# Later bounds of w_in and later tables of scales while attention runs alone

## The chip, the cores and the metric

The kernel runs on one core of a Trainium2 chip. The metric is the device time of one execution in microseconds (us), lower is better. The engines of a core work side by side, each through its own list of instructions in order: TensorE (PE in the profile; PEld is its weight load), VectorE (DVE), ScalarE (ACT), GpSimd (POOL), and SyncE (SP), which issues the DMAs.

## What is computed

Attention over 8 batches of 8 heads, followed by a feed-forward layer (FFN) on its output. Each head has 512 local and 32 global positions of 64 elements. Global queries see all keys; a local query sees the global keys and the local ones at most 32 places away.

```python
s_g = scale * q_g @ k_all.T;  out_g = sm(s_g) @ v_all
s_ll = where(|i - j| <= 32, scale * q_l @ k_l.T, -1e9)
out_l = sm(concat(scale * q_l @ k_g.T, s_ll)) @ concat(v_g, v_l)
x = concat(out_g, out_l)                  # 4608 tokens x 512
h = x @ w_in                              # 512 x 2048
g = where(h > 0, h, exp(min(h, 0)) - 1)
out = g @ w_out                           # 2048 x 512
```

## The kernel before

**Two streams.** attention() is a generator that issues the attention slot by slot; ffn_stream() issues the FFN for blocks of 256 tokens as they become ready. The main loop (the last lines of attn_ffn) takes one step of attention, and, by the table PACE, as many steps of the FFN as are due. For its first 66 steps attention runs alone: lead[0] is true, and the FFN stream issues no products. A slot has four steps, S, V, T and U. S computes scores (L685 and L689 for the global queries, L734 for the local ones), and the softmax follows: maxima on VectorE (L696 and L697, or L746), exponentials on ScalarE (L701, L703, L752), the reciprocal of the sum on VectorE (L756, L757), the product with it on GpSimd (L758, L710 for the global part). T, two slots later, transposes p on TensorE (L789) and copies it to the tile pt on VectorE (L791). U does the same for the global probabilities pg (L721 on TensorE, L722 on ScalarE, into the same pt). V, three slots later, multiplies pt with v (L795); ScalarE copies the output to xr (L828), and VectorE takes up the global part and the maximum (L833 or L835, L837). In the same steps, while attention is alone, L918 issues products of zeros on TensorE as fillers.

**The weights.** w_in and w_out come as 64-bit floats. They are turned into two float16 parts each, high and low, in units of 1 MB; unit(m, p, raw) does this for w_in (m = 0) or w_out (m = 1). Its pieces are put off by defer(n, fn): tick() counts steps, and fn is called n ticks later. s0 (L184 on ScalarE, L185 on GpSimd), s1a to s1c (L189, L192, L196 on VectorE) and s1d (L200 on ScalarE, which also gives each partition's maximum, the bound) rebuild 32-bit floats. For w_in, s2 spreads the bound over the partitions: all_max() transposes it on TensorE into a bank of PSUM (L137) and reduces it on VectorE (L138). s3 makes a power of two of it (L127, L128, L132) and writes the high part on ScalarE (L209, the tiles winh and wouth); s4 writes the low part on VectorE (L212, winl and woutl).

```python
lag = 7 if m else 16
for i, fn in ((1, s0), (1 + d, s1a), ..., (1 + 4 * d, s1d),
              (1 + lag, s2), (2 + lag, s3), (3 + lag, s4)):
    defer(i, fn)
```

**The tables.** When a group of weights has its last unit issued, load_weights() defers tables(group): L228 and L229 multiply the powers of w_in and w_out and take the maximum; five ticks later rest() spreads it by all_max (wm_a, wm_b) and makes the group's scales (L233, L234, L235). The FFN can start on a group when its tables exist; scales() (L579 to L583 on GpSimd) makes the scales of a block from them.

In the first 66 steps four units are issued, by UNITS: w_in and w_out of group a in steps 1 and 8, w_in and w_out of group b in steps 18 and 30. The later ones (groups c to e) are issued when, or shortly before, the FFN runs beside attention.

**What sets the order.** Engines work in order, but the order is set when the program is built: the Tile framework schedules by its own estimate of when an instruction can start, so that an operation that is deferred by a step can change places with several others. Tiles of the pool ps_a (named pa, four banks of PSUM) are shared by scores, transposes and all_max. Raw weights have two buffers, so that a load waits on SyncE's queue until L200 of the unit two before is done, and the loads of k, q and v behind it wait too.

Of the kernel before, what the change touches and what calls it, by code (L numbers as in the profile page):

```python
# [61 lines left out]
def attn_ffn(ctx: ExitStack, tc: tile.TileContext, qT, qgT, kT, vT, w_in, w_out, mask, out):  # L62
# [23 lines left out]
    def defer(n, fn):  # L86
        if n == 0:
            return fn()
        later.setdefault(now[0] + n, []).append(fn)
# [10 lines left out]
    lead = [True]  # L100
# [23 lines left out]
    def power(dst, src):  # L124

        dst = dst.bitcast(I32)
        nc.vector.tensor_scalar(dst, src.bitcast(I32), 0x7f800000, None, ALU.bitwise_and)  # L127
        nc.vector.tensor_scalar_max(dst, dst, LOW)  # L128

    def inverse(dst, src):  # L130

        nc.vector.tensor_scalar(dst.bitcast(I32), src.bitcast(I32), TOP, -1.0, ALU.subtract, ALU.mult)  # L132

    def all_max(dst, src):

        tp = ps_a.tile([P, 512], F32, name="pa")
        tc.keep_in_program_order(nc.tensor.transpose(tp[:, 0:P], src.to_broadcast([P, P]), ident))  # L137
        nc.vector.tensor_reduce(out=dst, in_=tp[:, 0:P], op=ALU.max, axis=AX.X)  # L138
# [15 lines left out]
    def load_weights():  # L154
        todo = [(group, m, p) for group in "abcde" for p in range(*GROUPS[group]) for m in range(2)]
        raws = [fetch(*todo[0][1:])]
        yield
        for n, (group, m, p) in enumerate(todo):
            if n + 1 < len(todo):
                raws.append(fetch(*todo[n + 1][1:]))  # L160
            unit(m, p, raws[n])
            if (m, p) == (1, GROUPS[group][1] - 1):
                defer(12, lambda group=group: tables(group))
                if p == NP - 1:
                    defer(13, lambda: tables("f"))
            yield

    def fetch(m, p):
        raw = ffn.tile([P, NC, 2 * P, 2] if m == 0 else [P, 2, DM, 2], I32, name="raw")
        nc.sync.dma_start(raw, w1[:, :, 2 * p * P:2 * (p + 1) * P, :] if m == 0 else w2[:, 2 * p:2 * p + 2, :, :])  # L170
        return raw

    def unit(m, p, raw):
        f = slice(2 * p * P, 2 * (p + 1) * P)
        shape = [P, NC, 2 * P] if m == 0 else [P, 2, DM]
        parts = [w[:, :, f] for w in win] if m == 0 else [w[:, 2 * p:2 * p + 2, :] for w in wout]
        pw = (pww if m == 0 else pwo)[:, p:p + 1]
        u = ffn.tile(shape, F32, name="cu", bufs=3)
        mx = ffn.tile([P, 4], F32, name="cm", bufs=4)
        high, low = raw[..., 1], raw[..., 0]  # L180
        ui = u.bitcast(I32)

        def s0():
            nc.scalar.activation(u, high.bitcast(F32), AF.Abs)  # L184
            nc.gpsimd.tensor_scalar(u, u, FMAX, FMIN, ALU.min, ALU.max)  # L185

        def s1a():
            tc.keep_in_program_order(
                nc.vector.tensor_scalar(ui, ui, 3, 0x3ffffff8, ALU.logical_shift_left, ALU.bitwise_and))  # L189

        def s1b():
            nc.vector.scalar_tensor_tensor(out=ui, in0=high, scalar=-0x40000000, in1=ui,  # L192
                                           op0=ALU.bitwise_and, op1=ALU.bitwise_or)

        def s1c():
            nc.vector.scalar_tensor_tensor(out=ui, in0=low, scalar=29, in1=ui,  # L196
                                           op0=ALU.logical_shift_right, op1=ALU.bitwise_or)

        def s1d():
            nc.scalar.activation(low.bitcast(F32), u, AF.Abs, accum_out=mx[:, m:m + 1])  # L200

        def s2():
            if m == 0:
                all_max(mx[:, 1:2], mx[:, 0:1])

        def s3():
            power(pw, mx[:, 1:2])
            inverse(mx[:, 3:4], pw)
            nc.scalar.activation(parts[0], u, AF.Copy, scale=mx[:, 3:4])  # L209

        def s4():
            nc.vector.scalar_tensor_tensor(out=parts[1].rearrange("p a b -> p (a b)") if m else parts[1],  # L212
                                           in0=u.rearrange("p a b -> p (a b)") if m else u, scalar=mx[:, 3:4],
                                           in1=parts[0].rearrange("p a b -> p (a b)") if m else parts[0],
                                           op0=ALU.mult, op1=ALU.subtract)

        d = 1 if lead[0] else 2
        lag = 7 if m else 16
        for i, fn in ((1, s0), (1 + d, s1a), (1 + 2 * d, s1b), (1 + 3 * d, s1c), (1 + 4 * d, s1d),
                      (1 + lag, s2), (2 + lag, s3), (3 + lag, s4)):  # L220
            defer(i, fn)

    def tables(group):

        r = slice(*GROUPS[group])
        wm = wts.tile([P, 4], F32, name=f"wm_{group}")
        t = wts.tile([P, NP], F32, name=f"t_{group}")
        nc.vector.tensor_mul(t[:, r], pww[:, r], pwo[:, r])  # L228
        nc.vector.tensor_reduce(out=wm[:, 0:1], in_=t[:, r], op=ALU.max, axis=AX.X)  # L229

        def rest():
            all_max(wm[:, 1:2], wm[:, 0:1])
            nc.vector.reciprocal(wm[:, 2:3], wm[:, 1:2])  # L233
            nc.vector.tensor_scalar(t[:, r], pwo[:, r], wm[:, 2:3], 8.0, ALU.mult, ALU.mult)  # L234
            nc.vector.tensor_scalar_mul(isc[:, r], pww[:, r], -2.0 ** -28)  # L235
            tab[group] = wm[:, 1:2], t

        defer(5, rest)
# [731 lines left out]

    f = ffn_stream()
    units = load_weights()
    done = credit = 0

# [108 lines left out]
```

## Time and profile before

| | us |
|---|---|
| three runs | 920.2, 917.78, 920.91 (median 920.2) |
| profiled execution | 918.45 |
| its span, first to last instruction | 916.6 |
| TensorE busy | 878.5 (96%) |
| VectorE busy | 703.1 (77%) |
| ScalarE busy | 637.2 (70%) |
| GpSimd busy | 177.4 (19%) |
| mean granted clock of TensorE | 0.996 |

A row of a time line gives start, duration, engine, line, operation, output and inputs, shapes, the number of merged instructions, and in brackets the idle time of the engine ahead of it with what ended it. A row of a stage gives its length, then busy time and number of instructions of PE, PEld, DVE, ACT and POOL, then the granted clock of TensorE (1.00 is full speed), the share of the DMA engines and GB/s. Numbers of buffers are left out in the profile, so that the tiles of different slots have one name.

### The profile page before, as it was taken

To read this page: it belongs to the slowest core of one execution; us is meant where nothing else is said; L and a number is where in the kernel's file an instruction comes from. 1 tells how busy PE (TensorE), PEld (TensorE's weight loads), DVE (VectorE), ACT (ScalarE), POOL (GpSimd) and SP (SyncE) were. 2 spreads that over 40 slices of the span, in tenths; PEclk is the share of its full clock that TensorE was granted. 3 is DMA by queue.
4 is the path that set the end of the run, shared out by engine and by line. 5 is a ranking of instruction groups with operands and counts; after the bars stand their busy time and mean duration, and the time that the engine had idled before them with its cause. 6 is when DMAs were issued, how large, how long until landed. Compare 5 with 4: busy or idle time off the path is not lost.

```text
span 916.6 us, 26268 instructions
## 1 busy us (share of the span) xinstructions
PE 878.5 (96%) x10791; PEld 719.0 (78%) x10791; DVE 703.1 (77%) x1949; ACT 637.2 (70%) x1458; POOL 177.4 (19%) x237
## 2 busy tenths in 40 slices
PE   7989888899999999999999999999999999999997
PEld 3557565566666888888888888888888888888886
DVE  5997998898689768686877768777868677766566
ACT  5789987876667667676767577676766676756664
POOL 3352554332212001011101011110110011200000
PEclk9899999999999999999999999999999999999999
DMA  7978866626643134104401134114410111000000
GB/s 264 369 267 286 292 210 219 200 89 210 196 144 103 71 128 154 50 24 130 174 24 51 70 128 154 50 60 138 154 35 37 48 48 48 1 25 24 1 25 24
DMA packets 41776, 108.32 MB, mean 118 GB/s; under 512 B 4152, under 2 KB 6840, under 8 KB 41656
## 3 DMA queue, kind: packets, MB, share of 16 engines
q1 hardware_dynamic: 41368, 106.38, 33.7%
q8 instruction: 85, 1.39, 0.6%
q14 instruction: 35, 0.29, 0.1%
q10 hardware_dynamic: 288, 0.26, 0.1%
HBM read 89.33 MB, written 17.30 MB: 116 GB/s over the span
## 4 chain that ended last, share of the span: by engine, by line
PE 33%; DVE 32%; ACT 25%; issue 4%; DMA 4%; POOL 0%; DVEq 0%; SPq 0%; ACTq 0%; POOLq 0%
PE pa L317 12%; ACT p L752 6%; ACT gh L355 6%; PE acc L476 6%; DVE gl L339 5%; DVE gx L336 5%; PE h L476 4%; ACT g L327 3%; ACT g L329 3%; DVE gx L350 2%; PE acc L441 2%; PE h L317 2%; DVE gx L351 2%; PE pa L795 2%; DVE cu L196 1%
## 5 line engine op out<-in xcount | busy, mean ns | idle before, releaser
L317 PEld LDWEIGHTS <-winh 128*128 128x128 f16 x2160 | 208.8, 98 | 32.4 <-issue 2.5
L317 PE MATMUL pa<-xh,winh 128*128 128x256 f16 x824 | 224.8, 273 | 1.4 <-DVE xglob L865 1.4
L317 PE MATMUL pa<-xh,winl 128*128 128x256 f16 x824 | 224.6, 273 | 0.0
L317 PE MATMUL pa<-xl,winh 128*128 128x256 f16 x824 | 224.6, 273 | 0.0
L355 ACT ACTIVATE gh<-gx,xs 128x896 f16<-128x896 f32 x103 | 107.5, 1044 | 133.3 <-DVE gx L352 133.3
L339 DVE SCALAR_TENSOR_TENSOR gl<-gx,xs,gh 128x896 f16<-128x896 f32 x103 | 122.6, 1191 | 73.8 <-ACT gh L355 73.8
L476 PEld LDWEIGHTS <-gh 128*128 128x128 f16 x1456 | 140.2, 98 | 19.5 <-issue 3.6
L758 POOL TENSOR_TENSOR p<-p,sm 128x512 f32<-128x512 f32 x64 | 71.4, 1118 | 330.0 <-DVE sm L757 301.8
L752 ACT ACTIVATE p<-p,m 128x128 f32<-128x128 f32 x256 | 99.3, 391 | 25.2 <-DVE m L746 25.0
L317 PEld LDWEIGHTS <-winl 128*128 128x128 f16 x1080 | 105.7, 98 | 12.6
L476 PE MATMUL acc<-wouth,gl 128*128 128x256 f16 x312 | 85.1, 273 | 1.2 <-DVE gl L339 1.1
L476 PE MATMUL acc<-wouth,gh 128*128 128x256 f16 x312 | 85.2, 273 | 0.0
L476 PE MATMUL acc<-woutl,gh 128*128 128x256 f16 x312 | 85.0, 273 | 0.0
L329 ACT ACTIVATE g<-g 128x512 f32<-128x512 f32 x135 | 85.0, 630 | 0.0
L476 PEld LDWEIGHTS <-gl 128*128 128x128 f16 x728 | 71.2, 98 | 11.5 <-DVE gl L339 3.3
L327 ACT ACTIVATE g<-pa,xs 128x512 f32<-128x512 f32 x103 | 70.2, 682 | 10.7 <-PE pa L317 10.0
L476 PE MATMUL h<-raw,gh 128*128 128x256 f16 x416 | 74.2, 273 | 0.0
L317 PE MATMUL h<-xh,winh 128*128 128x256 f16 x256 | 69.9, 273 | 0.0
L317 PE MATMUL h<-xl,winh 128*128 128x256 f16 x256 | 69.8, 273 | 0.0
L317 PE MATMUL h<-xh,winl 128*128 128x256 f16 x256 | 69.8, 273 | 0.0
L795 PEld LDWEIGHTS pa<-pt,v 128*64 128x64 f32 x1728 | 52.9, 138 | 8.0 <-issue 6.2
L336 DVE SCALAR_TENSOR_TENSOR gx<-g,p 128x512 f32<-128x512 f32 x52 | 35.9, 690 | 27.8 <-ACT g L329 26.3
(230 smaller groups left out, 1893.4 us busy)
## 6 DMA issues: line engine op xcount, KB each, us to landing
v<-vT SPq DMA_DIRECT2D x64, 512.0 KB, 4.5
k<-kT SPq DMA_DIRECT2D x32, 640.0 KB, 5.2
q<-qT SPq DMA_DIRECT2D x32, 256.0 KB, 5.8
raw<-w_in SPq DMA_DIRECT2D x8, 1024.0 KB, 5.6
raw<-w_out SPq DMA_DIRECT2D x8, 1024.0 KB, 5.9
od<-o SPq DMA_DIRECT2D x32, 256.0 KB, 2.6
o<-od SPq DMA_DIRECT2D x32, 256.0 KB, 3.0
out<-o SPq DMA_DIRECT2D x32, 256.0 KB, 2.3
```

Source lines behind the costliest of these rows:

```text
L317: nc.tensor.matmul(h[:, j, :], wt[:, c, f], xt[:, c, :], start=k == 0, stop=k == 11)
L327: nc.scalar.activation(g, hf, AF.Relu, scale=sc[:, p:p + 1])
L329: nc.scalar.activation(g, g, AF.Exp, scale=-1.0)
L336: nc.vector.scalar_tensor_tensor(out=out, in0=ins[0], scalar=-1.0, in1=ins[1], op0=ALU.add, op1=ALU.max)
L339: nc.vector.scalar_tensor_tensor(out=dst, in0=src, scalar=sg, in1=hi, op0=ALU.mult, op1=ALU.subtract)
L350: nc.vector.tensor_add(gx[:, 2:4, :], q[:, 0:2], q[:, 2:4])
L351: nc.vector.tensor_sub(gx[:, 5:7, :], q[:, 0:4:2], q[:, 1:4:2])
L355: nc.scalar.activation(gh, gx, AF.Copy, scale=sg)
L476: nc.tensor.matmul(cols, gt, w, start=p == 0 and k == 0, stop=last and k == len(todo) - 1, skip_group_check=True)
L752: nc.scalar.activation(ps[i], ps[i], AF.Exp, bias=m[:, i:i + 1], scale=-1.0, accum_out=s[:, 0, i:i + 1])
L758: nc.gpsimd.tensor_tensor(out=pp, in0=pp, in1=s[:, 1, :].unsqueeze(2).to_broadcast([P, 4, P]), op=ALU.mult)
L795: nc.tensor.matmul(o[:, to:to + n], st["v", g, t][:, 4 * h + w, :], st["pt", g, t][:, h, at:at + n], start=start, stop=True, skip_group_ch ...
```

## The change

While lead[0] is true, s2, s3 and s4 of a unit of w_in come six steps later (lag 22 in place of 16), and tables(group) eight steps later (20 in place of 12). This concerns the units of w_in of groups a and b and the tables of these two groups. s0 to s1d, the units of w_out and all units that are issued later keep their steps.

```diff
             if (m, p) == (1, GROUPS[group][1] - 1):
-                defer(12, lambda group=group: tables(group))
+                defer(20 if lead[0] else 12, lambda group=group: tables(group))
...
         d = 1 if lead[0] else 2
-        lag = 7 if m else 16
+        lag = 7 if m else 22 if lead[0] else 16
```

In the built program the order on SyncE is the same. On TensorE, VectorE, ScalarE and GpSimd it differs within attention's first 66 steps, and is the same behind them. Three places follow.

VectorE before, in the middle of attention's time alone. pt_676 is the copy of the transposed p of a slot of the first batch (the row at 40.76 us in the trace); cu_626 is the unit of w_out of group b, cm_402 the bound of w_in of group b:

```order
L756 TENSOR_SCALAR sm_591<-sm_591 128x4
L791 COPY pt_676<-pa_677 128x2x4x64
L757 RECIPROCAL sm_591<-sm_591 128x4
L189 TENSOR_SCALAR cu_626<-cu_626 128x1024
L138 TENSOR_REDUCE cm_402<-pa_683 128x1
L192 SCALAR_TENSOR_TENSOR cu_626<-raw_399,cu_626 128x1024
L127 TENSOR_SCALAR pww_114<-cm_402 128x1
L756 TENSOR_SCALAR sm_661<-sm_661 128x4
L196 SCALAR_TENSOR_TENSOR cu_626<-raw_399,cu_626 128x1024
```

VectorE now, at the same place. cu_620 is the same unit of w_out, pt_676 the same copy, and wm_a_559 the maximum for the tables of group a:

```order
L756 TENSOR_SCALAR sm_585<-sm_585 128x4
L746 ISA p1_84,m_654<-acc_637,msk_75 128x128
L746 ISA m_654 128x1
L757 RECIPROCAL sm_585<-sm_585 128x4
L138 TENSOR_REDUCE wm_a_559<-pa_660 128x1
L189 TENSOR_SCALAR cu_620<-cu_620 128x1024
L233 RECIPROCAL wm_a_559<-wm_a_559 128x1
L235 TENSOR_SCALAR isc_116<-pww_114 128x1
L192 SCALAR_TENSOR_TENSOR cu_620<-raw_396,cu_620 128x1024
L234 TENSOR_SCALAR t_a_560<-pwo_115,wm_a_559 128x1
L196 SCALAR_TENSOR_TENSOR cu_620<-raw_396,cu_620 128x1024
L791 COPY pt_676<-pa_677 128x2x4x64
```

The copy pt_676 has moved from ahead of L189, L192 and L196 of this unit to behind them.

TensorE now, around the product that reads pt_676 (h_725). pa_698 is the second bank of the scores of a later slot, p0_83 the next p to be transposed; k_632 belongs to the second batch:

```order
L734 MATMUL pa_698<-k_247,q_324 32x128 x4
L789 MATMUL pa_754<-ident_76,p0_83 128x128 x4
L795 MATMUL h_725<-pt_676,v_535 64x32 x2
L795 MATMUL h_725<-pt_676,v_535 64x64 x4
L795 MATMUL h_725<-pt_676,v_535 64x32 x4
L795 MATMUL h_725<-pt_676,v_535 64x64 x4
L795 MATMUL h_725<-pt_676,v_535 64x32 x2
L918 LDWEIGHTS wouth_91
L918 MATMUL h_749<-wouth_91 128x512
L721 MATMUL pa_766<-ident_76,pg1_82 128x128
```

Before, the product on pt_676 stood ahead of the transposes of p0_83, with a filler among its instructions; now it is behind them.

VectorE before, around the global maxima of the first batch's second half (mg_438):

```order
L229 TENSOR_REDUCE wm_a_416<-t_a_417 128x1
L235 TENSOR_SCALAR isc_116<-pww_114 128x1
L212 SCALAR_TENSOR_TENSOR woutl_92<-cu_227,cm_228,wouth_91 128x1024
L212 SCALAR_TENSOR_TENSOR winl_90<-cu_156,cm_157,winh_89 128x4x256
L696 TENSOR_REDUCE mg_438<-pa_424 128x1
```

Now, at the same place (mg_426):

```order
L757 RECIPROCAL sm_345<-sm_345 128x4
L138 TENSOR_REDUCE cm_157<-pa_480 128x1
L212 SCALAR_TENSOR_TENSOR woutl_92<-cu_227,cm_228,wouth_91 128x1024
L696 TENSOR_REDUCE mg_426<-pa_413 128x1
L696 TENSOR_REDUCE mg_426<-pa_412 128x1
```

winl of group a and the small steps ahead of it have gone from in front of the maxima; they stand now behind the maxima of the next two slots' local scores. The second winl (group b) stood in front of the maxima of the second batch, and is now behind them.

## The prediction

> **What bounds the kernel now.** I read the page first, then busy time by stage, then the time lines of VectorE (DVE), TensorE (PE), ScalarE (ACT) and GpSimd (POOL) in the stretch that the change touches, then the granted clock in windows of 3.41 us.
>
> The page: TensorE is busy nearly all the time, VectorE for three quarters.
>
> ```profile
> span 916.6 us, 26268 instructions
> PE 878.5 (96%) x10791; PEld 719.0 (78%) x10791; DVE 703.1 (77%) x1949; ACT 637.2 (70%) x1458; POOL 177.4 (19%) x237
> ```
>
> By stage (length, then busy time and instructions of PE, PEld, DVE, ACT, POOL, then granted clock, DMA share, GB/s):
>
> ```profile
> 30.00:69.00 39.00, 35.12 (x693) 23.27 (x693) 35.38 (x166) 30.14 (x109) 19.05 (x29) 1.00 0.84 307
> 200.00:400.00 200.00, 195.73 (x2356) 154.84 (x2354) 159.44 (x418) 134.98 (x324) 38.39 (x58) 1.00 0.37 123
> 400.00:916.00 516.00, 504.68 (x6217) 445.90 (x6215) 372.13 (x1015) 342.04 (x743) 53.35 (x73) 1.00 0.19 65
> ```
>
> From 200 us on TensorE is 98% busy (195.73 of 200; 504.68 of 516). Attention alone ends where the first FFN job stands:
>
> ```profile
> 68.89 0.27 PE L317 MATMUL h<-xh,winh 128*128 128x256 f16 x1
> ```
>
> Up to there many TensorE instructions are fillers (L918), and VectorE is the fullest engine doing needed work: 35.38 of 39.00 us from 30 on. Behind 69 us the change leaves the order of every engine as it is (SyncE's from the start, and the moved steps issue no DMA), and nothing there hangs on an absolute time: each transfer is issued when a buffer comes free. So what attention alone loses or gains I carry to the end one for one. The question is when the start ends.
>
> **Part 1: the bounds leave the stretch before 30 us.** The transpose that spreads the first bound of w_in is the place that the change seems to be about:
>
> ```profile
> 21.42 0.47 PE L137 MATMUL pa<-ident,cm 128*128 128x128 f32 x1 [1.58 <-ACT raw L200]
> 23.63 2.09 PE L685 MATMUL pa<-k,qg 64*32 64x256 f32 x8 [0.46 <-ACT pt L722]
> 30.01 0.42 PE L685 MATMUL pa<-k,qg 64*32 64x256 f32 x4
> ```
>
> TensorE waits 1.58 us for it. It would not start much earlier without it: what stands next, the transposes of p, needs GpSimd's p, which ends at 21.02 (19.02 + 2.00):
>
> ```profile
> 19.02 2.00 POOL L758 TENSOR_TENSOR p<-p,sm 128x512 f32<-128x512 f32 x1
> 41.70 1.30 POOL L758 TENSOR_TENSOR p<-p,sm 128x512 f32<-128x512 f32 x1 [1.09 <-DVE sm L757]
> ```
>
> So at most 0.4 us is won there, and it is lost again at 30 us: the second half of the global scores needs a block of k that is issued at 21.81 and takes 7.6 us.
>
> ```profile
> 30.01 0.12 PEld L685 LDWEIGHTS pa<-k,qg 64*32 64x32 f32 x4 [0.64 <-DMA k<-kT]
> ```
>
> ```profile
> 21.39 0.38 SPq L170 DMA_DIRECT2D raw<-w_in  x1
> 21.81 0.50 SPq L660 DMA_DIRECT2D k<-kT  x1
> ```
>
> ```profile
> k<-kT SPq DMA_DIRECT2D x1, 640.0 KB, 7.6
> ```
>
> That is 29.4 us, and the weight load behind it ends a wait for this DMA at 30.01. On SyncE's queue it stands behind the raw load of w_in, which goes out at 21.39, when L200 has left the buffer; the change moves neither. The maxima mg follow on VectorE at 30.78:
>
> ```profile
> 28.90 1.28 DVE L212 SCALAR_TENSOR_TENSOR winl<-cu,cm,winh 128x1024 f16<-128x1024 f32 x1
> 30.78 0.79 DVE L696 TENSOR_REDUCE mg<-pa 128x1 f32<-128x288 f32 x2 [0.60 <-PE pa L689]
> 40.76 0.68 DVE L791 COPY pt<-pa 128x512 f32<-128x512 f32 x1
> 41.45 0.66 DVE L189 TENSOR_SCALAR cu<-cu 128x1024 int32<-128x1024 int32 x1
> 42.23 1.86 DVE L192 SCALAR_TENSOR_TENSOR cu<-raw,cu 128x1024 int32<-128x1024 int32 x1
> 44.14 1.21 DVE L196 SCALAR_TENSOR_TENSOR cu<-raw,cu 128x1024 int32<-128x1024 int32 x1
> 45.28 0.14 DVE L128 TENSOR_SCALAR pww<-pww 128x1 int32<-128x1 int32 x1
> 49.63 0.42 DVE L696 TENSOR_REDUCE mg<-pa 128x1 f32<-128x256 f32 x1 [0.40 <-PE pa L689]
> ```
>
> Taking winl (1.28 us, at 28.90) away from before mg only lengthens the wait of 0.60 us in front of mg. Part 1 is worth **0**; bounds -0.4 (if k were not what is last) and +0.3 (the reduction of the moved cm transpose now precedes woutl, as long as winl, in front of mg).
>
> **Part 2: the same work comes back behind 30 us.** winl and six one-column steps (0.14 us each in the L128 row, overlapping) are now done between 36 and 42 us, where VectorE has little to spare (35.38 of 39.00). On ScalarE winh (1.1 us) now stands between the exponentials of two tiles and ahead of L184 of the next weight block. That L184 starts at 37.68:
>
> ```profile
> 37.30 0.39 ACT L752 ACTIVATE p<-p,m 128x128 f32<-128x128 f32 x1
> 37.68 1.16 ACT L184 ACTIVATE cu<-raw 128x1024 f32<-128x1024 f32 x1
> 46.71 1.13 ACT L209 ACTIVATE winh<-cu,cm 128x1024 f16<-128x1024 f32 x1
> ```
>
> I put it near 40.1: winh 1.1, three exponentials at 0.4 and a copy of 0.2 now stand ahead. GpSimd's clamp follows,
>
> ```profile
> 39.57 1.04 POOL L185 TENSOR_SCALAR cu<-cu 128x1024 f32<-128x1024 f32 x1
> ```
>
> then VectorE's L189, at 42.2 in place of 41.45: +0.7, which is inside the next part.
>
> **Part 3: the pt copy changes places with a weight block.** This is the term that decides. Before, the copy of 40.76 precedes L189, L192 and L196. Now, as the order shows, it is behind all three, and the values product on it stands on TensorE behind it:
>
> ```profile
> 42.35 0.31 PE L795 MATMUL h<-pt,v 128*64 128x32 f32 x4
> 43.85 0.39 PE L918 MATMUL h<-wouth 128*128 128x512 f16 x1
> 44.08 0.60 PE L789 MATMUL pa<-ident,p 128*128 128x128 f32 x4
> 44.52 0.38 PE L721 MATMUL pa<-ident,pg 128*128 128x128 f32 x2
> 44.74 0.81 PE L918 MATMUL h<-wouth 128*128 128x512 f16 x2
> 45.72 0.92 PE L685 MATMUL pa<-k,qg 64*32 64x256 f32 x8 [0.17 <-ACT pt L722]
> 47.55 1.12 PE L795 MATMUL h<-pt,v 128*64 128x32 f32 x32 [0.90 <-issue]
> 48.92 0.42 PE L685 MATMUL pa<-k,qg 64*32 64x256 f32 x4
> ```
>
> From 42.2: L189 0.6, L192 1.1 (its 1.86 less what it loses to GpSimd), L196 1.1, small steps 0.2, and one GpSimd product of about 1.0 that VectorE has to sit out. The last is read from the rows: the L192 of 42.23 took 1.86 us while GpSimd's p ran from 41.70 to 43.00; the L196 of 44.14, alone, 1.21. Sum 4.0: the copy starts at 46.2 (45.2 without a collision, 47.2 with a second one, with the next clamp). [...]
>
> The values product then starts at 46.9 in place of 42.35. From there to mg TensorE does, by starts in the rows: the product 1.05 (47.55), four fillers at 0.23 (43.85 to 44.08), the transposes of pg 0.22, eight L685 0.92, nine sixteenths of the next product 0.6, and the last L685 and L689 0.65. Sum 4.4, so mg starts at 51.3 instead of 49.63: **+1.6** at full clock. Before, the product had 5.2 us until the next one; part of its 4.5 us of lateness goes into that slack.
>
> **Part 4: the clock.** While the copy is late, TensorE has little to do. In windows of 3.41 us, set on the edge where the clock fell:
>
> ```profile
> 17.91:21.32 3.41, 1.45 (x30) 0.99 (x29) 3.41 (x6) 2.19 (x8) 3.11 (x2) 1.00 0.03 10
> 21.32:24.73 3.41, 2.85 (x13) 1.61 (x15) 3.41 (x13) 1.86 (x8) 1.51 (x1) 0.50 0.64 171
> 24.73:28.15 3.42, 3.42 (x35) 2.28 (x37) 3.07 (x17) 2.93 (x6) 1.60 (x2) 0.50 1.04 412
> 41.80:45.21 3.41, 3.35 (x59) 2.44 (x58) 3.41 (x6) 1.88 (x6) 1.21 (x1) 1.00 1.01 406
> 133.96:137.37 3.41, 1.70 (x11) 0.84 (x9) 3.41 (x5) 3.39 (x5) 0.00 (x0) 1.00 0.52 152
> ```
>
> 1.45 us of work in a window was followed by 6.83 us at half clock; 1.70 was not. The window from 41.80 holds 3.35 now. After the change the values product (about 1.1) and what stood behind it (L721 and L918, 0.9) leave it; what stays is the second bank of scores (0.6, it waits until wm_a's bank is read near 42.1), part of the first, and four transposes (0.5), and from 43.7 to 46.9 TensorE has nothing. That is 1.0 to 1.3 us in any such window, below 1.45: I expect the clock to halve, once, at 45 to 47 us, until about 52. At half clock the L685 of 23.63 took 2.09 where the one of 45.72 took 0.92. The 4.4 us from the product to mg stretch by at most 2.6 (5.1 us at half rate), by 1.0 if the drop comes late. I take **+2.0**.
>
> [...]
>
> **Part 5: the rest of the start.** The second winl, before it in front of the mg of 49.63, comes behind that mg and ahead of a pt copy; winh stands ahead of four exponentials. Against that VectorE has waits left, like the 0.40 us in front of 49.63, in which small steps vanish. -0.2, bounds -0.8 and +0.8. The tables of group b end later, just ahead of the last pt copies of the start; GpSimd's scales with wm_b wait for them, and a pg product is queued behind. The first FFN job, at 68.89, needs group a's scales alone: 0, covered by the job of group a; if that cover is gone, the 1 us of a GpSimd product.
>
> **The sum.** 0 + 1.6 + 2.0 - 0.2 = **+3.4**. The profiled execution took 918.45 us, 916.6 of it span. The runs shown are 920.2, 917.78 and 920.91, mean 919.6; I set the sum on that mean: **923.0**. Without part 4 it is +1.4: 921.0.
>
> **Rivals.**
> - The clock stays up (24%). Speaks for it: where the windows' edges fall differs, and the product of GpSimd may not collide. Time 921.0 (920.2 to 922).
> - Nothing is seen (8%): VectorE's waits of 3.6 us between 30 and 69 take up the 1.6 us of moved work. Time 919.6.
> - Faster (16%): the start is shorter, because TensorE no longer waits 1.58 us behind the bound, the window that ends at 21.3 is fuller than 1.45 and the clock does not fall there. At half clock the rows of 23.63 and those up to 28.1 lose some 3 us; this counts only if k's landing at 29.4 and mg at 30.78 do not hold the start, and if the copy of part 3 is ready in an idle slot of VectorE. It decides from about 2.2 us won ahead of the copy. Time 916.6 (915 to 918.6).
> - Forecast (52%): 923.0, own range 921.8 to 925.1.
>
> 0.3% (2.8 us) is about what can be told from no change here. Slower by more: seven eighths of the forecast and a little of the first rival, 0.49; faster: two thirds of the fast rival, 0.10; same 0.41. Range 918.5 to 925.5.
>
> **What would show it.** In the changed profile: mg of the first batch still at 30.7 to 31.1, ahead of it a longer wait of VectorE; the pt copy that was at 40.76 at 45 to 47.5; a stretch of half clock between 44 and 53; the second mg at 53 (51.3 if the clock stays); the first L317 at 72 instead of 68.89, and the same distance from there to the end. I am wrong if mg of the first batch moves forward, if the copy comes before 43, or if the distance behind the first L317 changes by more than 1 us.

## The result and the profile after

The changed kernel takes 928.96 us (median of 926.02 to 930.95), the kernel before 920.2: ratio 1.0101, 95% interval 1.0084 to 1.0118. It is slower, as forecast, but by some 9 us where the prediction had 3.4, and the time lies above the range. Timed again the ratio was 1.0091 (1.0075 to 1.0108).

The page of the profiled execution, which took 928.96 us:

```profile
span 927.1 us, 26271 instructions
PE 887.8 (96%) x10791; PEld 722.9 (78%) x10791; DVE 706.1 (76%) x1949; ACT 637.8 (69%) x1458; POOL 177.1 (19%) x237
```

The first FFN job has moved from 68.89 to 79.14 us, 10.25 us, and the end by 10.5 (916.6 to 927.1). So the loss lies in the start, where the prediction looked for it. By stage, to be held against the rows of before (columns as there):

```profile
30.00:79.14 49.14, 41.61 (x698) 26.06 (x697) 41.05 (x173) 32.25 (x112) 18.27 (x29) 0.88 0.70 250
...
400.00:927.00 527.00, 515.22 (x6314) 455.56 (x6311) 380.50 (x1034) 350.59 (x760) 55.45 (x78) 1.00 0.19 64
```

From 30 us on TensorE needs 49 us for what it did in 39, is less full (85% instead of 90%), and the granted clock is 0.88 where it was 1.00.

TensorE at the end of the first stretch and at the first FFN job, after:

```profile
30.48 0.42 PE L137 MATMUL pa<-ident,cm 128*128 128x128 f32 x1
...
31.55 0.60 PE L789 MATMUL pa<-ident,p 128*128 128x128 f32 x4
...
32.08 0.42 PE L685 MATMUL pa<-k,qg 64*32 64x256 f32 x4
...
79.14 0.27 PE L317 MATMUL h<-xh,winh 128*128 128x256 f16 x1
```

The transposes of cm and of p now stand ahead of L685, and it starts 2.07 us later than before (30.01). The block of k is not what it waits for: issued at 22.79, it landed after 6.4 us, at 29.2.

```profile
22.79 0.50 SPq L660 DMA_DIRECT2D k<-kT  x1
```

```profile
k<-kT SPq DMA_DIRECT2D x1, 640.0 KB, 6.4
```

VectorE from the first mg to the second:

```profile
32.78 0.79 DVE L696 TENSOR_REDUCE mg<-pa 128x1 f32<-128x256 f32 x2
...
40.55 1.78 DVE L212 SCALAR_TENSOR_TENSOR winl<-cu,cm,winh 128x1024 f16<-128x1024 f32 x1
...
44.35 0.26 DVE L138 TENSOR_REDUCE wm_a<-pa 128x1 f32<-128x128 f32 x1
...
44.53 0.68 DVE L189 TENSOR_SCALAR cu<-cu 128x1024 int32<-128x1024 int32 x1
...
45.25 1.94 DVE L192 SCALAR_TENSOR_TENSOR cu<-raw,cu 128x1024 int32<-128x1024 int32 x1
...
47.23 1.93 DVE L196 SCALAR_TENSOR_TENSOR cu<-raw,cu 128x1024 int32<-128x1024 int32 x1
...
49.08 0.68 DVE L791 COPY pt<-pa 128x512 f32<-128x512 f32 x1
...
56.23 0.79 DVE L696 TENSOR_REDUCE mg<-pa 128x1 f32<-128x256 f32 x2 [2.51 <-PE pa L689]
```

The copy of pt stands behind L189, L192 and L196, at 49.08 in place of 40.76, and none of the three waits: VectorE goes from winl to the copy without a pause. TensorE waits meanwhile, first 1.10 us for the bank that wm_a holds, then 0.85 for p, then 3.00 for the copy:

```profile
44.66 0.64 PE L734 MATMUL pa<-k,q 64*32 64x128 f32 x16 [1.10 <-DVE wm_a L138]
...
46.16 0.66 PE L789 MATMUL pa<-ident,p 128*128 128x128 f32 x4 [0.85 <-POOL p L758]
...
49.81 1.92 PE L795 MATMUL h<-pt,v 128*64 128x32 f32 x32 [3.00 <-DVE pt L791]
...
55.04 0.56 PE L795 MATMUL h<-pt,v 128*64 128x32 f32 x10
```

A product of this shape took 1.12 us before (at 47.55); this one takes 1.92: half clock. Windows of 3.41 us, set on or close to the edges where the clock changed (the column behind POOL's is the granted clock):

```profile
14.02:17.43 3.41, 1.55 (x42) 1.16 (x42) 1.40 (x4) 3.41 (x15) 2.45 (x3) 1.00 1.02 400
17.43:20.85 3.42, 3.31 (x33) 1.73 (x35) 3.42 (x7) 2.46 (x8) 2.39 (x2) 0.50 0.12 40
...
24.26:27.68 3.42, 2.22 (x18) 1.03 (x12) 2.74 (x8) 2.10 (x6) 2.00 (x1) 0.50 1.03 384
27.68:31.10 3.42, 3.42 (x38) 2.52 (x35) 1.00 (x6) 2.65 (x4) 1.44 (x2) 0.50 1.02 407
...
44.80:48.20 3.40, 1.16 (x20) 0.65 (x14) 3.40 (x6) 1.45 (x4) 3.05 (x2) 1.00 1.02 397
48.20:51.60 3.40, 1.78 (x32) 1.79 (x32) 3.14 (x13) 1.59 (x4) 1.04 (x1) 0.50 0.11 39
...
68.60:72.00 3.40, 2.05 (x32) 1.37 (x27) 3.28 (x22) 2.64 (x13) 2.03 (x4) 1.00 0.86 340
72.10:75.50 3.40, 3.40 (x55) 2.42 (x52) 1.56 (x5) 2.06 (x5) 2.28 (x9) 0.50 0.52 151
```

Half clock lasts from 17.4 to 31.1, from 48.2 to 55.0 and from 72.1 to 75.5: 23.9 us up to the first FFN job, where before had 6.8 (21.3 to 28.1). This pair of profiles shows the clock's part larger than it is on average: the profiled execution of before has a mean granted clock of 0.996, while the runs of before average 0.992 to 0.994 beside the experiments, and those of the changed kernel 0.986 and 0.987. Four marks divide the start, in us of each profile: the first row of each mg, the first L317 and the end. Where a woutl or an xl stands between the two reductions of an mg (e3, e10, e11, e13 and e14 at the second, e1 and e15 at the third), the other reduction comes 1.5 to 2.2 us later. The last column is the median's distance to before, by the ratio and its interval times 919.6 us:

| kernel | first mg | to second mg | to third mg | to first L317 | to end | over before |
|---|---|---|---|---|---|---|
| before | 30.78 | 18.85 | 9.58 | 9.68 | 847.7 | |
| changed | 32.78 | 23.45 | 10.65 | 12.26 | 848.0 | 9.3 (7.7 to 10.9) |
| changed, second time | 32.78 | 23.80 | 10.65 | 11.01 | 845.9 | 8.4 (6.9 to 9.9) |
| e1, tables only | 32.08 | 18.52 | 9.66 | 12.72 | 847.1 | 2.7 (1.7 to 3.7) |
| e2, tables six steps | 32.02 | 21.38 | 9.99 | 10.66 | 846.1 | 5.2 (3.9 to 6.6) |
| e3, copy early | 32.71 | 19.73 | 10.23 | 11.01 | 846.6 | 4.4 (2.9 to 6.0) |
| e4, fillers at the copy | 32.82 | 21.29 | 10.78 | 11.00 | 846.8 | 6.7 (4.4 to 8.9) |
| e5, before, copy late | 31.00 | 20.79 | 12.88 | 9.27 | 846.6 | 3.9 (2.4 to 5.2) |
| e6, fillers at the start | 29.98 | 23.73 | 10.65 | 11.01 | 846.2 | 6.3 (4.6 to 7.9) |
| e7, before, fillers | 30.75 | 19.15 | 9.58 | 9.68 | 848.8 | -0.1 (-1.2 to 1.0) |
| e9, wm_b later | 32.35 | 23.25 | 10.65 | 11.19 | 847.0 | 7.8 (6.1 to 9.5) |
| e10, e3 and e9 | 32.76 | 19.73 | 10.23 | 11.18 | 846.6 | 3.7 (2.2 to 5.1) |
| e11, e10 and e6 | 30.16 | 20.77 | 10.24 | 11.18 | 848.3 | 2.1 (1.0 to 3.2) |
| e12, e4 and e6 | 30.27 | 21.32 | 10.77 | 12.29 | 848.6 | 6.9 (5.4 to 8.4) |
| e13, e11, scales on VectorE | 30.48 | 19.77 | 10.23 | 10.51 | 848.4 | 1.9 (0.9 to 2.9) |
| e14, tables five steps | 30.20 | 19.58 | 10.57 | 10.49 | 848.7 | 1.4 (0.4 to 2.5) |
| e15, e1, scales on VectorE | 31.73 | 18.54 | 9.67 | 11.61 | 847.5 | 2.5 (1.6 to 3.4) |

Of the 10.5 us in the profile, 2.0 are lost up to the first mg, 4.6 up to the second, 3.65 up to the first FFN job, 0.25 behind it.

### The profile page after: what moved, and what is told of

Its sections match the earlier page's. It is cut to its first block, busy times and chain, and to the rows that moved or that the text cites. A ratio compares the mean times of both kernels' runs of the same rounds, so it can differ in the third digit from the quotient of the medians.

```text
span 927.1 us, 26271 instructions
## 1 busy us (share of the span) xinstructions
PE 887.8 (96%) x10791; PEld 722.9 (78%) x10791; DVE 706.1 (76%) x1949; ACT 637.8 (69%) x1458; POOL 177.1 (19%) x237
## 4 chain that ended last, share of the span: by engine, by line
PE 34%; DVE 32%; ACT 25%; issue 4%; DMA 3%; POOL 0%; DVEq 0%; ACTq 0%; POOLq 0%
PE pa L317 12%; ACT p L752 6%; ACT gh L355 6%; PE acc L476 6%; DVE gl L339 5%; DVE gx L336 5%; PE h L476 4%; ACT g L327 3%; PE acc L441 3%; ACT g L329 3%; DVE gx L350 2%; PE h L317 2%; DMA raw<-w_out 2%; DVE gx L351 2%; PE pa L795 2%
## 5 line engine op out<-in xcount | busy, mean ns | idle before, releaser
L317 PEld LDWEIGHTS <-winh 128*128 128x128 f16 x2160 | 209.0, 98 | 32.7 <-issue 3.1
L317 PE MATMUL pa<-xh,winh 128*128 128x256 f16 x824 | 224.8, 273 | 1.4 <-DVE xglob L865 1.4
L317 PE MATMUL pa<-xl,winh 128*128 128x256 f16 x824 | 224.6, 273 | 0.0
L317 PE MATMUL pa<-xh,winl 128*128 128x256 f16 x824 | 224.6, 273 | 0.0
L317 PEld LDWEIGHTS <-winl 128*128 128x128 f16 x1080 | 105.7, 98 | 12.7
L317 PE MATMUL h<-xh,winh 128*128 128x256 f16 x256 | 70.0, 273 | 0.0
L317 PE MATMUL h<-xl,winh 128*128 128x256 f16 x256 | 69.8, 273 | 0.0
L317 PE MATMUL h<-xh,winl 128*128 128x256 f16 x256 | 69.8, 273 | 0.0
```

Source lines behind the costliest of these rows:

```text
L317: nc.tensor.matmul(h[:, j, :], wt[:, c, f], xt[:, c, :], start=k == 0, stop=k == 11)
```

## The experiments

**The theory and its rivals.** The theory at the outset: the copy of pt behind the weight block starves TensorE, and the starving halves its clock. Rivals: the tables alone; the moved winl and winh wherever the copy stands; the clock alone.

**e1, the tables alone.** Before, with

```
-                defer(12, lambda group=group: tables(group))
+                defer(20 if lead[0] else 12, lambda group=group: tables(group))
```

> The kernel before with only the tables of the scales eight steps later; w_in's bounds are spread where they were. My theory (the copy of pt behind w_out's VectorE block starves TensorE, and the starving halves the clock) and the rival that w_in's winl and winh are what costs both expect no change: 919 to 922, the copy at 40.8, the first FFN job at 69. A theory in which the late tables are the cost (group b's tables end ahead of the last pt copies of the start, where part 5 of the prediction measured 3.65 us that it did not expect) expects 922 to 925 and a first FFN job at 71 to 73.

Measured: 921.53, 2.7 over before, which took 918.99 beside it. The time lies inside the theory's 919 to 922, but the distance to before and the first FFN job at 72.98 are those of the other theory: the late tables have a price of their own, which the prediction had set at nothing. The clock does not make it, as the granted clock of the runs averages 0.994 in both. TensorE at the end of e1's start:

```profile
60.84 0.27 PE L137 MATMUL pa<-ident,wm_b 128*128 128x128 f32 x1
...
63.60 0.44 PE L721 MATMUL pa<-ident,pg 128*128 128x128 f32 x2 [1.26 <-DVE pt L791]
...
72.27 0.66 PE L789 MATMUL pa<-ident,p 128*128 128x128 f32 x4 [0.97 <-POOL p L758]
...
72.98 0.27 PE L317 MATMUL h<-xh,winh 128*128 128x256 f16 x1
```

Two waits that before does not have (its largest there is 0.65 us): the transposes of pg wait until a pt copy lets go of a bank, after wm_b has taken one, and the last transposes of p wait for GpSimd. Together 2.2 us, against 3.04 more between the third mg and L317. A further 1.3 us are lost up to the first mg of this profile, behind a half clock from 16.3 to 30.0, though w_in's bounds stand where before has them.

**e2, tables six steps later.** The changed kernel with

```
-                defer(20 if lead[0] else 12, lambda group=group: tables(group))
+                defer(18 if lead[0] else 12, lambda group=group: tables(group))
```

> The changed kernel with the tables six steps later in place of eight: nearly only the bounds are later, and the pt copy stands ahead of L196 and behind L189 and L192. My theory: the copy is late by 3.5 to 6.5 us instead of 8.3, so a part of the loss is left: 924 to 928, and a clock that may or may not drop at 45 to 48. The rival that the moved winl and winh cost what they cost wherever the copy stands expects the whole loss, 928 to 930. If the tables were the cost it would be back near 920 to 922.

Measured: 923.98, 5.2 over before. The copy came at 46.13, behind L189 and L192 only, and the way from the first mg to the second is 2.1 us shorter than in the changed kernel: a copy that is less late goes with a smaller loss. Half clock is shorter there too (46.6 to 50.1), and the tables are two steps earlier, so this run does not give the copy's part alone. The rival of the moved work alone, which expected 928 to 930, falls.

**e3, the copy early.** The changed kernel with

```
+            with tc.high_priority(offset=30 if (st["b"], g, t) == (0, 1, 0) else 0):
                 copy(pt.rearrange("p h (a x) -> p a h x", x=HQ)[:, 0:3:2], ...
```

> The changed kernel with one instruction moved: the copy of pt for tile (b 0, g 1, t 0) again ahead of w_out's VectorE block. My theory: the copy at 40 to 42, TensorE busy at 43 to 49, no half clock there, the second mg less than 20 us behind the first, and most of the loss gone: 921 to 924 (the half clock from 17.4 to 31 is ahead of the copy and keeps its 1 to 2 us). The rival that the cost is the amount of work moved behind 30 us, whatever its order: 927 to 930. The rival that it is the clock alone: the drop at 48 goes and with it 2 to 3 us, the rest stays: 925 to 927.

Measured: 922.44, 4.4 over before. VectorE of e3 (L792 is L791 elsewhere):

```profile
42.86 0.67 DVE L792 COPY pt<-pa 128x512 f32<-128x512 f32 x1
...
52.44 0.42 DVE L696 TENSOR_REDUCE mg<-pa 128x1 f32<-128x256 f32 x1 [0.89 <-PE pa L689]
```

First to second mg 19.73 instead of 23.45 to 23.8, and no half clock from 32 us to the first FFN job. So one instruction's place, with what follows from it (woutl at 52.78 now stands between the two reductions of mg), is worth 4 to 5 us (4.4 over before in place of 8.4 to 9.3), about half of the loss. The other half is elsewhere.

**e4, the clock held up while the copy is late.** The changed kernel with 18 more fillers:

```
-                    for _ in range(IDLE if i == 1 + LAGT else 2):
+                    for _ in range(IDLE if i == 1 + LAGT else 20 if (i, what) == (9, "V") else 2):
```

> The changed kernel with 20 filler matmuls in place of 2 at the step where TensorE stands idle for want of the late copy; the copy stays late. It tells the wait from the clock. If the clock is the whole cost of the late copy, the drop at 48 goes, the second mg is back at 51 to 52 and the time is 922 to 925. My theory has both: the drop goes, about 2 us with it, and the late copy keeps its own wait: 926 to 927. If the fillers hold up needed work themselves: 929 or more.

Measured: 925.37, 6.7 over before. The profile shows no half clock from 31.1 us to the first FFN job (one follows at 123.3). The product starts where it did and runs at full rate:

```profile
49.12 0.68 DVE L791 COPY pt<-pa 128x512 f32<-128x512 f32 x1
...
49.90 1.12 PE L795 MATMUL h<-pt,v 128*64 128x32 f32 x32 [1.39 <-issue]
...
54.11 0.79 DVE L696 TENSOR_REDUCE mg<-pa 128x1 f32<-128x256 f32 x2 [1.10 <-PE pa L689]
```

First to second mg 21.29: of the 4.6 us that the changed kernel loses there, 2.2 are the clock and 2.4 the wait. So in these profiles the drop follows the late copy, and is about half of its price.

**The changed kernel again** (e8), without an edit, beside the next three.

> The changed kernel, once more, as the anchor for the parts run on other chips. All theories expect what was measured: 8 to 11 us over before. It also shows how the granted clock and the time go together from run to run: if the clock is most of the loss, runs with a clock above 0.99 are within 4 us of before; if the order of the work is most of it, they are not below 5.

Measured: 927.81, clock 0.984 to 0.990 over the runs, none below 925.9. No run here had a clock above 0.990; one of the first five had 0.992, and its 926.02 is 5.8 over before's 920.2. That speaks for the order of the work as the larger part. In its profile the clock falls at 21.7 rather than 17.4 and not at all at 72; the first mg is at 32.78 all the same.

**e5, before with the copy late.**

```
+            with tc.high_priority(offset=-40 if (st["b"], g, t) == (0, 1, 0) else 0):
                 copy(pt.rearrange("p h (a x) -> p a h x", x=HQ)[:, 0:3:2], ...
```

> The kernel before with one copy of pt (tile b 0, g 1, t 0) put behind w_out's VectorE block; bounds and tables are where they were, though woutl comes ahead of the second mg with it. My theory (the place of this copy is the largest term): 3 to 6 us over before, the copy at 45 to 47, the values product behind it. If the copy only hurts together with winl and wm_a ahead of it: 0 to 2 us over before. If it is the clock alone: a drop between 44 and 53 in the profile and 2 to 3 us, or no drop and no loss.

Measured: 923.38, 3.9 over before, with half clock from 45.3 to 55.6. A late copy, with bounds and tables where they were, makes about the loss that the prediction had for it (3.6). It came at 45.8, its product behind it. Other steps moved with it (woutl ahead of the second mg), so the place of the loss is spread: 1.9 us up to the second mg, 3.3 from there to the third.

**e6 and e7, fillers at the start.** In the changed kernel, and in the kernel before:

```
-                    for _ in range(IDLE if i == 1 + LAGT else 2):
+                    for _ in range(IDLE if i == 1 + LAGT else 8 if (i, what) == (4, "T") else 2):
```

> The changed kernel with 6 more fillers on TensorE between the first values product and the second set of transposes of p, in the gap in front of 21 us behind which the clock falls. If the half clock from 17.4 to 31 is what brings the first mg to 32.8 in place of 30.8, the first mg comes at 31 to 31.8 and the time falls by 1 to 2 us. If the new order on TensorE (the transposes of p and cm ahead of the second half of the global scores) is it, the first mg stays at 32 or later and the time stays within 1 us of the changed kernel. If the fillers hold up needed work: slower by 1 us.

> The kernel before with the same 6 fillers. The window that ends at 21.3 was 1.45 us full and the clock fell; with the fillers it is fuller. If the clock then stays up from 21 to 28: 1 to 3 us faster than before, 916 to 918, a version that beats both. If the k transfer holds the first mg at 30.8 whatever the clock: the same as before within 0.5 us. If the clock falls all the same and the fillers run at half rate ahead of the transposes: 1 us slower.

Measured: e6 925.41, 6.3 over before and 2.4 under the changed kernel beside it; e7 919.52, no difference from before. In e6's profile the clock stays up until 46.0, and

```profile
29.98 0.79 DVE L696 TENSOR_REDUCE mg<-pa 128x1 f32<-128x256 f32 x2 [0.21 <-PE pa L689]
```

the first mg is 2.8 us earlier than in the changed kernel and 0.8 earlier than before. So in this order, without half clock at the start, nothing is lost up to the first mg. In e7 a half clock of 6.8 us remains, only earlier (15.9 to 22.7), and the first mg is where it was.

**e9, e10, e11, e12: do the terms add?** e9 spreads wm_b three steps later, behind the transposes of pg:

```
-        defer(5, rest)
+        defer(8 if group in "b" else 5, rest)
```

e10 has this and e3's edit, e11 e6's fillers besides, e12 the fillers of e4 and e6 alone.

> The changed kernel with one step moved: the bound of group b's scales (wm_b) is spread three steps later still, so that TensorE does the transposes of pg ahead of it. My theory of the stretch from the second mg to the first FFN job: wm_b's transpose takes a PSUM bank that the transposes of pg then wait for (1.35 us behind a pt copy), so that wait goes and the time falls by about 1.3 us, to 7 to 8 over before. If what costs there is the lateness of the scales, or GpSimd's queue behind them: slower than the changed kernel by 0.5 us or more. If neither: the same as the changed kernel within 0.5 us.

> The changed kernel with two steps moved: the pt copy ahead of w_out's block again, and wm_b three steps later. If the terms add: 8.5 less about 4.5 (the copy with its half clock) less 1.3 (the bank) is 2 to 3.5 over before. If the terms were one and the same loss seen twice: 4 to 4.5 over before, what the early copy alone gave.

> The same with the 6 fillers ahead of 21 us besides. If the three terms (half clock at the start, copy, bank) are the whole loss: 0 to 1 over before, with the first mg at 30 to 31, the second at 50 and the first FFN job near 70. If the moved work itself (winl and six small steps in the stretch where VectorE is full) has a price of its own that no order hides: 2 to 3 over before. If the bound out of the way is a gain once nothing else goes wrong: below before.

> The changed kernel with fillers at both places where TensorE starves (6 ahead of 21 us, 18 while it waits for the late copy), so that the clock stays up in most runs; the order of the needed work is that of the changed kernel. What is left over before is then the order alone. If the order alone is some half of the loss, as the copy's wait of about 2.5 us and the bank's of 1.35 say: 3.5 to 5 over before. If the clock is nearly all: 0 to 2. If it is the order that counts and the clock little: 7 or more.

Measured: e9 927.58, e10 922.92, e11 922.22, e12 926.77. e9's 7.8 over before lies inside what the theory of the bank expected, but also within the interval of the changed kernel (6.9 to 9.9), and the stages do not show the 1.3 us: as a price of its own the bank was a miss. TensorE in the changed kernel's second profile waits at one place behind the third mg, in e9's at two others:

```profile
70.34 0.44 PE L721 MATMUL pa<-ident,pg 128*128 128x128 f32 x2 [1.35 <-DVE pt L791]
```

```profile
69.41 1.13 PE L795 MATMUL h<-pt,v 128*64 128x32 f32 x32 [0.68 <-PE acc L734]
...
76.73 0.66 PE L789 MATMUL pa<-ident,p 128*128 128x128 f32 x4 [1.25 <-POOL p L758]
```

The wait of 1.35 us is gone, and 11.01 us have become 11.19: the product of p on GpSimd, which stands behind the scales that wait for wm_b, is late next. e10 is not better than e3 beyond the intervals. e11 brings the loss down to 2.1 us, the lowest of these, so the start's clock and the copy seem to add (its interval overlaps e10's). They are not the whole loss: for that 0 to 1 was expected, and 2 to 3 if the moved work has a price of its own. The clock is not up throughout even here: e11's profile has half clock from 21.1 to 24.5 and, with the copy early, from 48.4 to 51.8. e12 is no better than e4 or e6 alone, and its 3.5 to 5 were a miss. In its profile the clock falls at 16.2, and at 67.4, 122.0 and 152.7 besides; but over its runs the granted clock averages 0.992, and that of before beside it 0.993. So fillers at one place or at both bring the loss from 8.4 to 9.3 down to 6.3 to 6.9, and with a clock nearly that of before most of it is still there. That part is order, as far as the fillers themselves cost nothing; e7 shows it for those at the start.

**e13, e14, e15: what is left.** In e13 (e11 with this edit) and e15 (e1 with it) the scales of the first two blocks go to VectorE:

```
-            nc.gpsimd.tensor_scalar(sc[:, r], isc[:, r], mx[:, 2:3], 1.0, ALU.mult, ALU.mult)
+            eng.tensor_scalar(sc[:, r], isc[:, r], mx[:, 2:3], 1.0, ALU.mult, ALU.mult)
...
```

where eng is nc.vector in the first four calls of scales(). e14 is the changed kernel with e6's fillers, e3's edit, and the tables at 17 in place of 20.

> The kernel with all three repairs (fillers at the start, copy early, wm_b three steps later), and with the scales of the first two blocks computed by VectorE, so that GpSimd's p product has no scales ahead of it. If GpSimd's queue is what is left: the wait of 1.25 us in front of the last transposes of p goes, third mg to first FFN job 10 us in place of 11.2, and the time is 0 to 1.2 over before. If the sixteen steps on VectorE (about 0.1 us each) cost what they save: 2 to 3 over, as without them.

> The changed kernel with fillers at the start and the copy early, and the tables five steps later than before in place of eight, which is as early as the late bounds allow; wm_b is then spread ahead of the third mg. If the lateness of the tables is what is left (2.7 us for eight steps): 0 to 1.5 over before. If the moved winl, winh and small steps are: 2 to 3 over, with second mg to third mg still half a microsecond or more above before's 9.6.

> The kernel before with only the tables eight steps later, and the scales of the first two blocks on VectorE. If GpSimd's queue makes most of the 2.7 us of late tables: 0.5 to 1.5 over before. If it is the bank that wm_b's transpose holds (1.26 us in that kernel's profile) and the order on VectorE, with xl between the two reductions of the third mg: 2 to 3 over.

Measured: e13 921.30, e14 921.08, e15 921.42. GpSimd's queue falls as the one cause, as neither e13 (1.9 over, after 2.1) nor e15 (2.5, after 2.7) is better beyond the intervals: in e13 its wait is gone and TensorE waits for VectorE instead, in e15 the wait of the bank is still there:

```profile
70.12 0.38 PE L919 MATMUL h<-wouth 128*128 128x512 f16 x1 [0.80 <-DVE xglob L836]
```

```profile
63.09 0.44 PE L722 MATMUL pa<-ident,pg 128*128 128x128 f32 x2 [1.08 <-DVE pt L792]
```

e14 has the smallest loss of the versions with late bounds, 1.4 us (0.4 to 2.5), and its first mg 0.6 us ahead of before: that much is won at the change's own place in this profile, and more is lost behind. No version is faster than the kernel before.

## Why the prediction was right in its sign and wrong in its size

**Part 1 (0, bounds -0.4 and +0.3) is the first step that failed: it was worth 2.0 us up to the first mg.** I had the block of k hold L685 at 29.4. In the changed kernel it lands at 29.2 and nothing waits for it; TensorE, at half clock until 31.1, still has transposes of pg, cm and p ahead. I had quoted the row of 1.45 us that the clock fell behind, and treated the half clock as a given length. It is not: in before the window 24.73 to 28.15 was full (3.42) and the clock came back; in the changed kernel's second profile it fell at 21.7, nearly where it fell before, and the next windows read

```profile
21.69:25.10 3.41, 2.51 (x15) 1.01 (x13) 3.41 (x13) 1.98 (x8) 1.55 (x1) 0.51 0.60 181
25.10:28.52 3.42, 2.84 (x36) 2.50 (x36) 2.09 (x8) 1.97 (x5) 1.01 (x2) 0.50 1.04 419
28.52:31.93 3.41, 3.35 (x15) 1.88 (x11) 1.64 (x2) 1.99 (x4) 1.60 (x2) 0.50 1.04 407
```

so it stays down one window longer (two in the first profile). In this second profile TensorE gets past the place of the bound sooner and waits there for p instead, which before it did not:

```profile
25.68 1.11 PE L789 MATMUL pa<-ident,p 128*128 128x128 f32 x4 [1.48 <-POOL p L758]
```

e6 shows the counter-test: with the gap filled the first mg is at 29.98, and 2.4 us of the loss are gone. How much of the 2.0 us is the change's own is not shown: e1 and e15, whose bounds stand where before has them, had half clock from 16.3 to 30.0 and from 15.9 to 29.5, and their first mg came at 32.08 and 31.73. Where the clock falls varies from profile to profile, and that of before has a short stretch.

**Parts 2 and 3 were right.** The copy was to come at 46.2, which is 15.4 us behind the first mg; it came 16.3 behind. Of the 0.9, some 0.7 is the second collision with GpSimd, which I had as the upper end: L192 and L196 took 1.94 and 1.93 us, both beside a product or clamp of GpSimd (the L196 of before at 44.14, with GpSimd idle from 43.00 to 45.49, took 1.21),

```profile
44.60 1.50 POOL L758 TENSOR_TENSOR p<-p,sm 128x512 f32<-128x512 f32 x1 [0.49 <-DVE wm_a L138]
...
46.33 1.75 POOL L185 TENSOR_SCALAR cu<-cu 128x1024 f32<-128x1024 f32 x1 [0.23 <-ACT cu L184]
```

**Part 4 was right.** The clock fell once while the copy was late, from 48.2 to 55.0 (forecast 45 to 47 until about 52, with 2.0 us of start to add), behind a window with 1.16 us of work (forecast 1.0 to 1.3). From the product to mg took 6.42 us, forecast 4.4 + 2.0. Parts 3 and 4 together: 3.6 forecast, 4.6 in the profile, 3.9 over before when the copy is made late in the kernel before (e5).

**Part 5 (-0.2, bounds -0.8 and +0.8; late tables 0) is the second step that failed: 2.4 us in one profile, 3.65 in the other.** Of both, 1.07 are lost between the second and the third mg, where e1 with late tables alone loses 0.08: that points at the second winl and winh, for which I had -0.2, but no run takes it apart. The rest, 1.33 and 2.58 from the third mg to L317, is where the late tables act. e1 shows 2.7 for the tables alone. I had seen that GpSimd's scales and a pg product stand behind wm_b, and taken the first FFN job's need as the only one. What is queued behind the scales in e1 and e9 is the product of p, and what wm_b's transpose takes, in the changed kernel too (1.35), is a bank; attention needs both before that job. The 3.65 also holds a third half clock, 72.1 to 75.5, which the second profile does not have (12.26 against 11.01 from the third mg to L317).

**"One for one" held in the profile (847.7 and 848.0 behind L317), but only there.** In the second profile it was 845.9: of the 9.35 us by which L317 was late, 1.9 came back by the end, more than the 1 us that I had named as a sign of being wrong. The first profile has one more half clock behind L317, from 177.9 to 181.3, which the second does not have, so that its 848.0 is in part luck. No run was made on why the rest is shorter.

**The rivals.** That the clock stays up (24%) did not come true; e4 and e6 show what it would have given at each place. That the place of the fall differs is seen: 17.4 and 21.7 us for the first one in the two profiles of the changed kernel. "Nothing is seen" (8%) lies outside both intervals. "Faster" (16%) had a true half: with a fuller window the first mg is 0.8 us ahead (e6), but the start is held by what comes behind. The range was too narrow because I took the bounds of parts 1 and 5 from rows of VectorE and of a DMA, the engines that I thought last, and none from TensorE's clock or its banks.

**What stays open.** With the copy early, fillers at the start and wm_b spread at another step, 1.4 to 2.1 us are left (e11, e13, e14), though half clock up to L317 is then 6.8 us in each profile, as in before. Each wait that was taken away (bank 1.35, product of p 1.25) gave way to others (0.68 and 1.25, then 0.80), so none of them was seen to be the one cause. The stages of the three profiles say where it is: 0.7 to 1.9 us between the first and the second mg, 0.7 to 1.0 from there to the third, and 0.8 to 1.5 from there to L317, against 0.3 to 0.6 won ahead of the first.

## What to carry to other kernels

Where the order on the engines is made when the program is built, a step is not moved alone: here bounds and tables moved by six and eight steps put one PSUM copy behind 4.55 us of VectorE work (44.53 to 49.08), and that copy was about half the loss. Where TensorE is paced by others, price a change also by the time that the clock stays down (here one to four windows of 3.41 us), not just by the gap ahead of the fall, and take more than one profile of it. And of a small step that is made late, look at what it holds meanwhile (a bank, for which TensorE waited 1.35 us here; the head of a queue, 1.25 us in e9), not only at who needs its result.

## What was not expected of the hardware

- The clock came back behind windows with 3.19 (e2) to 3.42 us (before) of work, but so full a window was not always enough: at half clock, windows with 2.22 (changed), 2.51 and 2.84 (its second profile) and 2.85 (before) did not bring it back, nor did one with 3.31 (changed, 17.43 to 20.85 above), nor in e5 one with 3.42. It fell behind windows with 1.16 and 1.55 (changed) and 1.45 (before), and once in the changed kernel behind one with 2.05 (68.6 to 72.0), while windows with 1.51 (e6, 11.9 to 15.3) and 1.70 (before, 133.96 to 137.37) left it up. So in these profiles the amount of work alone does not decide; what else does was not found. The return behind 3.19 in e2, and the full window that stayed low in e5, each with the window behind it:

```profile
46.64:50.06 3.42, 3.19 (x37) 2.51 (x38) 3.37 (x15) 1.23 (x2) 1.54 (x2) 0.50 0.34 126
50.06:53.47 3.41, 3.30 (x40) 1.37 (x38) 1.16 (x7) 3.09 (x12) 1.04 (x1) 1.00 0.40 142
```

```profile
48.71:52.13 3.42, 3.42 (x28) 1.04 (x27) 2.31 (x6) 2.30 (x7) 0.00 (x0) 0.50 0.54 153
52.13:55.54 3.41, 3.41 (x30) 1.97 (x30) 1.43 (x4) 0.00 (x0) 1.04 (x1) 0.50 0.72 246
```

- The stretches of half clock last 3.4 (e10, e11), 6.8 (before), 10.2 (changed, second profile) or 13.7 us (changed), multiples of the window of 3.41 us within 0.1. In the changed kernel the falls at 17.4, 48.2 and 72.1 lie 9 and 7 windows apart, and in its second profile those at 21.7 and 49.0 lie 8 apart; but the first falls of these two profiles are 4.3 us apart, which is no multiple. The first one begins between 15.1 (e10) and 21.7 us in profiles whose instructions up to there are the same or nearly so (with fillers there at 46.0 in e6, but at 16.2 in e12). What sets its place was not found.
- A one-column step of GpSimd, 0.27 us in the rows around it, took 1.29 when VectorE had begun a 1.28 us product (xl) just ahead of it, and ended 0.14 us behind that product (e1):

```profile
68.89 1.28 DVE L566 SCALAR_TENSOR_TENSOR xl<-xr,xm,xh 128x1024 f16<-128x1024 f32 x1
...
69.02 1.29 POOL L579 TENSOR_SCALAR xs<-isc,xm 128x1 f32<-128x1 f32 x1
```
